# Fused attention and a two-layer feed-forward block: attention ahead of two passes of seven block products that share PSUM banks

## The chip, the cores and the metric

The kernel runs on one NeuronCore of a Trainium2 chip, as one program. The metric is device time in microseconds (us) of one execution, the median of three runs: 921.73 us for the kernel before (920.55 to 922.61). Everything is computed in fp32 or in pairs of fp32r halves.

## The reference

```python
scores = cap * np.tanh((q @ k.T / sqrt(64)) / cap)      # 4 batches x 12 heads, 448 x 64
attn = exp(scores - max); attn /= attn.sum(-1) + 1e-9
x = concat_heads(attn @ v)                              # (4, 448, 768)
u = x + ((x.T @ U @ V).T)                               # mixing over the 448 tokens, rank 32
out = u + np.maximum(u @ w_ch1, 0) @ w_ch2              # w_ch1 768 x 3072, w_ch2 3072 x 768
```

The weights U, V, w_ch1 and w_ch2 arrive as 64-bit floats and are turned into fp32 on the chip.

## The kernel before

A small planner inside the program makes a list of tasks (each with an engine or a choice of two, a duration, a priority, and the buffers it uses), plays them through in time, and writes the instructions out in the order found. So every engine gets a fixed queue, and what the planner was told (durations, latencies, priorities, begin times, pools of buffers) sets the order. A task that may go to ScalarE (ACT) or VectorE (DVE) is given to one of them there.

**Attention** (`two`, `normalize`, `mixin`) goes in 12 steps of two head pairs (four heads). Scores (line 396) are 64-row fp32 products, two at a time on TensorE (PE); ACT takes tanh (401) and exp (409); the products with v (436) and the product for the last 64 keys (423, "rest") go into `o` banks; DVE adds the exponentials (445), PE sums them over partitions (475), and the reciprocal makes a round trip through DRAM on the POOL queue (480, 485, 498) before u is scaled (502). `mixin` transposes u (525), multiplies with U (540) and V (561) and adds (565). PE works in another shape ("mode") for scores, rest, products with v, sums, and everything else. q is scaled on DVE (376). `ALONE = 12` lets the first six steps use extra PSUM banks; the other six begin at planned times (`FROM`, `PACE`) among the feed-forward work.

**The feed-forward part** (`moe`) makes two passes over the 3072 hidden columns in 12 chunks of two blocks of 128. Pass 0 serves batches 0 and 1, pass 1 batches 2 and 3. Every product is three fp32r matmuls (high x high, high x low, low x high) of 448 columns.
- In pass 0, `up_plain` (738) takes 18 matmuls for each of 2 blocks x 2 batches: 72 a chunk.
- In pass 1, `up_seven` (759) multiplies the 2 x 2 blocks of batches and hidden columns by seven block products (Winograd's form of Strassen's scheme): 63 a chunk. The operand sums are made by `operands` and `strassen_weights` (lines 590, 597). Each product gets a PSUM bank of its own; ACT copies two out (229) and DVE does five adds from PSUM (771) and two in SBUF (776).
- `down` (823) takes 72 matmuls a chunk, 6 for each of 12 output tiles, and DVE adds each bank to u (828), 288 adds in all.
- Relu leaves two halves in `g` (229, 723).
- `block` and `convert`: in pass 0 a raw 64-bit block is loaded (623, two `wr` buffers) and made fp32 by one ACT instruction (270) and three DVE instructions (274, 279, 283); the result is used and also stored to DRAM (627, `kept`). Pass 1 loads it from there (617). DVE and ACT split each block into halves (654, 229).

At the end of pass 1 the 12 outputs are sent to DRAM (834).

Of the kernel before, what the change touches and what calls it, by code (L numbers as in the profile page):

```python
# [11 lines left out]
F32 = mybir.dt.float32  # L12
F32R = mybir.dt.float32r
# [6 lines left out]
DM = H * D  # L20
# [13 lines left out]
ALONE = 12  # L34

PACE = 50000
FROM = 90000
# [27 lines left out]
LAT = {"PE": 240, "ACT": 110, "DVE": 110, "POOL": 150, "SP": 0}  # L65
SWITCH = 95


class Plan:
# [43 lines left out]
    def simulate(self):  # L113
# [11 lines left out]
        def room(b):  # L125
            if self.order[b.tag][head[b.tag]] is not b:
                return None
            for p in b.pools:
                if p.free[b.tag] and all(not q.due for q in p.after):
                    return p  # L130
            return None

        def can(t, e):
            if any(b.pool is None and not room(b) for b in t.bufs):
                return False
# [10 lines left out]
        def start(t, e):  # L146
# [6 lines left out]
            cost = t.durs[e] + (SWITCH if t.mode != mode[e] else 0)  # L153
# [11 lines left out]
        while True:  # L165
            for e in LAT:
                if free[e] <= now and ready[e]:
                    for t in sorted(ready[e], key=lambda t: (t.prio, t.i)):
                        if can(t, e):
                            start(t, e)  # L170
                            break
            if not events:
                break
# [61 lines left out]

class Build(Plan):
    def __init__(self, tc, qk, v, u, vv, w1, w2, cap, ident, out):
# [7 lines left out]
        self.wp = Pool("wp", {"wa": 2, "w1": 3, "g": 3})  # L245
        self.wq = Pool("wq", {"wr": 2, "w0": 2})
        self.pre = Pool("pre", {"th": 4, "qk": 1, "es": 2})
        self.hp = Pool("hp", {"hl": 2}, after=(self.pre,))
        self.ap = Pool("ap", {"qk": 3, "vn": 2, "th": 3, "es": 2, "sr": 1, "r7": 2, "rb": 2, "xh": 1, "xl": 1, "ys": 1},
            side="right")  # L250
        self.xp = Pool("xp", {"x": 4, "ws": 3, "g": 3, "wa": 1}, after=(self.hp, self.wq))
        self.late = Pool("late", {"x": 3, "ws": 4, "cx": 4, "ta": 3}, after=(self.ap,), side="right")
        self.px = Pool("px", {"sc": 1, "s": 1}, space=PSUM, side="right")
        self.ps = Pool("ps", {"sc": 1, "o": 1, "misc": 2}, space=PSUM)
        self.pm = Pool("pm", {"mm": 3}, after=(self.px,), space=PSUM, side="right")
        self.pl = Pool("pl", {"mm": 5}, after=(self.ps,), space=PSUM)
        self.dp = None


    def convert(self, raw, raw_t, a, a_t, prio, n):  # L260

        nc = self.nc
        k = n / 768
# [4 lines left out]
        def low():  # L272
            half = raw_t().bitcast(U16)
            nc.vector.tensor_scalar(  # L274
                out=half[:, 0::4], in0=half[:, 1::4], scalar1=13, scalar2=None, op0=ALU.logical_shift_right)
# [10 lines left out]

        self.task({"ACT": 900 * k}, absolute, r=[(raw, "u")], w=[(a, 0)], prio=prio)
        self.task({"DVE": 1040 * k}, low, r=[(raw, "l")], w=[(raw, "l0")], prio=prio)
        self.task({"DVE": 1040 * k}, sign, r=[(raw, "u"), (raw, "l0")], w=[(raw, "l1")], prio=prio)
        self.task({"DVE": 960 * k}, join, r=[(raw, "l0"), (raw, "l1"), (a, 0)], w=[(a, 0)], prio=prio, lock=True)  # L290


    def consts(self):
# [6 lines left out]
        nc.vector.tensor_scalar(out=self.qsc, in0=self.qsc, scalar1=1.0 / D ** 0.5, scalar2=None, op0=ALU.mult)  # L300
        self.ident = pool.tile([128, 128], F32, name="ident")
# [5 lines left out]
    def mixing_consts(self):  # L307
        nc = self.nc
        begin, prio = 4000, -150
        raw = self.buf("wr", [128, 2 * DM], I32, self.wq)  # L310
        raw2 = self.buf("wr", [128, 2 * DM], I32, self.wq)
        a, a2 = (self.buf("wa", [128, DM], F32, self.wp) for _ in range(2))
# [25 lines left out]
        self.task({"DVE": 800}, u_parts, r=[(a, 0)], w=[("ust", 0)], prio=prio)  # L338
        self.convert(raw2, lambda: raw2.t[:, :2 * S], a2, lambda: a2.t[:, :S], prio, S)
        self.task({"DVE": 900}, v_parts, r=[(a2, 0)], w=[("vst", 0)], prio=prio)  # L340


    def attention(self):

        self.u_bufs = [self.buf("u%d" % b, [128, NP, S], F32, self.up) for b in range(B)]
        for p in range(0, B * NP, 2):
            self.two(p)
            self.normalize(p + 1)  # L350
            self.mixin(p // NP, p % NP // 2)

    def psum(self, tag, p, n=1):
        pools = {"sc": (self.ps, self.px), "s": (self.px,)}.get(tag) if p < ALONE else None
        tag = "misc" if tag == "s" and not pools else tag
        return self.buf(tag, [128, 512] if n == 1 else [128, n, 512], F32, *(pools or (self.ps,)))

    def begin(self, p):
        return 0 if p < ALONE else FROM + (p - ALONE) // 2 * PACE

    def two(self, p):


        nc = self.nc
        b, prio = p // NP, p - 100
        begin = self.begin(p)
        pools = (self.ap, self.pre) if p < ALONE else (self.ap,)
        vn = self.buf("vn", [128, 7, 2, D], F32, self.ap)
        qks = [self.buf("qk", [128, 2, S], F32, *pools) for _ in range(2)]
        for i, qk in enumerate(qks):  # L370

            def load(i=i, qk=qk):
                nc.sync.dma_start(out=qk.t, in_=self.qk[b, p % NP + i])

            def scale(qk=qk):
                nc.vector.tensor_scalar(out=qk.t[:, 0], in0=qk.t[:, 0], scalar1=self.qsc, scalar2=None, op0=ALU.mult)  # L376

            self.task({"SP": 350}, load, w=[(qk, 0)], lat=3600, prio=prio, begin=begin)
            self.task({"DVE": 560}, scale, r=[(qk, 0)], w=[(qk, 0)], prio=prio)
# [513 lines left out]
```

## Time and profile before

| what | value |
|---|---|
| median of three runs | 921.73 us |
| the profiled execution: span | 921.8 us |
| PE busy | 898.0 us (97%) |
| DVE busy | 714.1 us (77%) |
| ACT busy | 379.9 us (41%) |
| matmuls, attention and mixing / pass 0 / pass 1 | 1080 / 1728 / 1620 |
| mean granted PE clock | 0.992 of 2.4 GHz |

The profile is of one execution. Busy time is the union of an engine's instructions; a matmul's record is longer than the time until the next can start, so the chain's pieces, which run from start to start, are the better price of a group of matmuls. The span of the profile and the median of the runs agree to 0.1 us.

### The profile page before, as it was taken

How to read it: one execution, taken by the hardware profiler on the slowest of the kernel's cores; microseconds unless marked ns; L12 is line 12 of the kernel's file. 1: busy time of each engine (PE TensorE's matmuls, PEld its weight loads, DVE VectorE, ACT ScalarE, POOL GpSimd, SP SyncE). 2: the span in 40 equal slices, each digit the busy share in tenths (PEclk: the TensorE clock that was granted, in tenths of full speed). 3: DMA queues.
4: the chain of work that ended last, by engine and by line, in shares of the span. 5: the costliest groups of instructions: out<-in, count | busy, mean ns of one | idle time of the engine just before them, and what ended most of it. 6: DMA issues, size and time to landing. Idle time of an engine off the chain costs nothing.

```text
span 921.8 us, 11491 instructions
## 1 busy us (share of the span) xinstructions
PE 898.0 (97%) x4428; PEld 704.5 (76%) x4428; DVE 714.1 (77%) x1119; ACT 379.9 (41%) x513; POOL 60.5 (7%) x112
## 2 busy tenths in 40 slices
PE   6999999999999998999999999899999999999998
PEld 2233375767767666599999998799999999999997
DVE  5798896887887876778898775977777777777755
ACT  6988755545354541724323232512332222332210
POOL 0322210101011111020000000000000000000000
PEclk9999999999999998999999999999999999999999
DMA  7546330545434426145445433221121121122103
GB/s 255 173 153 204 92 101 32 163 175 169 167 125 149 138 61 211 66 137 181 121 156 190 163 103 123 100 72 67 52 69 56 48 61 60 52 69 67 38 1 120
DMA packets 34262, 104.58 MB, mean 113 GB/s; under 512 B 6192, under 2 KB 10272, under 8 KB 34208
## 3 DMA queue, kind: packets, MB, share of 16 engines
q1 hardware_dynamic: 23072, 79.29, 27.6%
q10 hardware_dynamic: 6912, 18.88, 5.1%
q0 software_dynamic: 4224, 5.68, 2.2%
q8 instruction: 35, 0.57, 0.3%
q14 instruction: 19, 0.16, 0.1%
HBM read 79.28 MB, written 24.47 MB: 113 GB/s over the span
## 4 chain that ended last, share of the span: by engine, by line
PE 90%; DMA 4%; DVE 4%; issue 1%; ACT 1%; POOL 0%; SPq 0%; DVEq 0%; POOLq 0%
PE mm L823 37%; PE mm L738 18%; PE mm L759 15%; PE sc L396 7%; PE o L436 4%; PE misc L436 2%; PE o L423 2%; PE misc L540 2%; DMA qk<-in_qk 1%; PE misc L525 1%; DMA r<-sr 1%; DMA rb<-rd 1%; DMA rd<-r 1%; PE misc L561 1%; PE misc L475 1%
## 5 line engine op out<-in xcount | busy, mean ns | idle before, releaser
L823 PE MATMUL mm<-g,w 128*128 128x448 f32 x1728 | 376.3, 368 | 0.5 <-DVE g L723 0.4
L823 PEld LDWEIGHTS mm<-g,w 128*128 128x128 f32 x1728 | 322.3, 188 | 44.5 <-issue 8.2
L828 DVE TENSOR_TENSOR u<-u,mm 128x448 f32<-128x448 f32 x288 | 177.7, 622 | 54.5 <-PE mm L823 50.5
L738 PE MATMUL mm<-hl,w 128*128 128x448 f32 x864 | 189.4, 371 | 0.0
L738 PEld LDWEIGHTS mm<-hl,w 128*128 128x128 f32 x864 | 160.2, 189 | 28.9 <-issue 14.9
L759 PE MATMUL mm<-x,ws 128*128 128x448 f32 x756 | 166.4, 368 | 3.7 <-DVE ws L597 3.6
L759 PEld LDWEIGHTS mm<-x,ws 128*128 128x128 f32 x756 | 142.4, 189 | 16.9 <-DVE ws L597 4.4
L401 ACT ACTIVATE th<-sc 128x896 f32<-128x896 f32 x84 | 75.2, 917 | 57.5 <-PE sc L396 43.4
L396 PE MATMUL sc<-qk 64*128 64x448 f32 (+1 forms) x384 | 87.1, 595 | 7.3 <-DVE qk L376 6.1
L229 ACT ACTIVATE w<-wa 128x768 fp32r<-128x768 f32 x72 | 59.4, 838 | 57.3 <-PE mm L823 35.7
L409 ACT ACTIVATE th<-th,capt 128x1792 f32<-128x1792 f32 (+1 forms) x48 | 76.7, 1603 | 0.7
L771 DVE TENSOR_TENSOR cx<-cx,mm 128x448 f32<-128x448 f32 x60 | 37.2, 620 | 45.8 <-PE mm L759 45.8
L654 DVE TENSOR_TENSOR w<-wa,w 128x768 fp32r<-128x768 f32 x72 | 68.6, 952 | 1.3 <-ACT w L229 0.3
L270 ACT ACTIVATE wa<-wr 128x768 f32<-128x768 f32 (+2 forms) x50 | 44.8, 896 | 55.7 <-DVE w L654 43.1
L274 DVE TENSOR_SCALAR wr<-wr 128x768 uint16<-128x768 uint16 (+2 forms) x50 | 50.6, 1024 | 17.1 <-DMA wr<-in_w 14.9
L396 PEld LDWEIGHTS sc<-qk 64*128 64x128 f32 (+1 forms) x384 | 27.1, 178 | 41.9 <-issue 14.7
L445 DVE TENSOR_TENSOR es<-es,th 128x896 f32<-128x896 f32 (+1 forms) x48 | 52.1, 1084 | 6.8 <-ACT th L409 6.3
L229 ACT ACTIVATE ws<-ta 128x384 fp32r<-128x384 f32 x39 | 20.3, 523 | 75.6 <-PE mm L759 69.3
L279 DVE TENSOR_SCALAR wr<-wr 128x768 uint16<-128x768 uint16 (+2 forms) x50 | 50.7, 1022 | 0.2
L229 ACT ACTIVATE g<-mm 128x448 fp32r<-128x448 f32 x48 | 26.1, 543 | 60.1 <-PE mm L738 60.1
L436 PE MATMUL o<-th,vn 128*64 128x448 f32 x216 | 47.5, 561 | 3.3 <-ACT th L409 3.0
L283 DVE SCALAR_TENSOR_TENSOR wa<-wa,wr 128x768 int32<-128x768 int32 (+2 forms) x50 | 46.5, 931 | 2.6 <-ACT wa L270 2.4
(77 smaller groups left out, 597.3 us busy)
## 6 DMA issues: line engine op xcount, KB each, us to landing
wr<-in_w SPq DMA_DIRECT2D x48, 768.0 KB, 5.5
kept<-wa ACTq DMA_DIRECT2D x48, 384.0 KB, 5.7
wa<-kept SPq DMA_DIRECT2D x48, 384.0 KB, 3.1
qk<-in_qk SPq DMA_DIRECT2D x24, 448.0 KB, 5.8
vn<-in_v SPq DMA_DIRECT2D x12, 448.0 KB, 7.3
rb<-rd POOLq DMA_DIRECT2D x48, 112.0 KB, 3.8
out_t<-u SPq DMA_DIRECT2D x24, 224.0 KB, 1.9
r<-sr POOLq DMA_DIRECT2D x48, 1.8 KB, 2.7
```

What stands on the lines that cost most here:

```text
L229: e.activation(out=out, in_=in_, func=func)
L279: nc.vector.tensor_scalar(out=half[:, 1::4], in0=half[:, 3::4], scalar1=0x8000, scalar2=None, op0=ALU.bitwise_and)
L396: nc.tensor.matmul(ps.t[out, a, :S], qks[c].t[hd, 1, 128 * t:min(S, 128 * t + 128)], qks[c].t[hd, 0], start=True, stop=True)
L401: nc.scalar.activation(out=th.t[:, j], in_=ps.t[:, :, :S], func=AF.Tanh)
L409: nc.scalar.activation(out=th.t[:, :n], in_=th.t[:, :n], func=AF.Exp, scale=self.capt)
L436: nc.tensor.matmul(o.t[64 * a:64 * a + 64, :S], vn.t[:, 3 * i + t, a], th.t[:, j, a], start=t == 0 and not late, stop=t == 2 and late)
L445: e.tensor_tensor(out=out(), in0=in0(), in1=in1(), op=ALU.add)
L654: e.tensor_tensor(out=w.t[:, 1], in0=a.t, in1=w.t[:, 0].bitcast(F32), op=ALU.subtract)
L738: nc.tensor.matmul(ps.t[:, :S], w.t[:, wi, sl], hl.t[:, xi, d], start=d == 0 and i == 0, stop=d == ND - 1 and i == 2)
L759: nc.tensor.matmul(ps.t[:, :S], ws[p].t[:, wi, sl], xs[p].t[:, xi, d], start=n == 0, stop=n == 8)
L823: nc.tensor.matmul(ps.t[:, :S], w1[f].t[:, wi, sl], g[b, f].t[:, gi], start=f == fs[0] and i == 0, stop=f == fs[-1] and i == 2)
L828: nc.vector.tensor_tensor(out=u.t[:, d], in0=u.t[:, d], in1=ps.t[:, :S], op=ALU.add)
```

## The change

- **Order.** All 12 attention steps come first with the extra banks (`ALONE = 22`), the begin times are gone, and mixing runs two steps behind (`LAG`). The planner's durations and latencies are replaced, a change of PE's mode has a price of its own, and among PE tasks within two priorities of the best one that keeps the mode is taken (`NEAR`).
- **Attention.** q is not scaled on DVE; tanh takes the scale. The rest product is one task for both head pairs in all steps.
- **Passes.** Both passes use `up_seven`. Products 1, 6, 7 and 4 are accumulated in one PSUM bank (`chain`) and products 5 and 3 in a second; the bank is read between them: three ACT copies and three DVE adds from PSUM a chunk, and one relu directly from the bank.
- **Down.** 3 of the 12 output tiles (`STAY`) keep a PSUM bank for the whole pass and are added to u once, at its end: 222 adds in all. Five banks are left for the others.
- **Weights.** `converted` runs as its own stream, begun at 9 us and planned no closer than 7 us apart, with one `wr` and one `wc` buffer (two in the first eight blocks); the low part may be made on ACT (`FLOOR`). Both passes load the blocks from DRAM.

```diff
-ALONE = 12
-PACE = 50000
-FROM = 90000
+ALONE = 22
+LAG = 2
+STAY = 1, 5, 9
+FIRST = 8
+START, PACE = 9000, 7000
+NEAR = 2
...
+        self.cv = Pool("cv", {"wr": 1, "wc": 1})
+        self.pre = Pool("pre", {"th": 4, "qk": 1, "es": 2, "wr": 1, "wc": 1})
...
+        self.pl = Pool("pl", {"mm": 5 - len(STAY), "acc": len(STAY)}, after=(self.ps,), space=PSUM)
...
-                    nc.scalar.activation(out=th.t[:, j], in_=ps.t[:, :, :S], func=AF.Tanh)
+                    nc.scalar.activation(out=th.t[:, j], in_=ps.t[:, :, :S], func=AF.Tanh, scale=self.qsc)
...
-        if late:
-            self.task({"PE": 760}, lambda: rest((0, 1)), r=[(vn, 0), (rth, rj)], w=[(o, 0) for o in os], prio=prio, mode="ar")
+        self.task({"PE": 760}, rest, r=[(vn, 0), (rth, rj)], w=[(o, 0) for o in os], prio=prio, mode="ar")
...
-            xs = self.operands(bs) if n else {b: self.halves(b) for b in bs}
+            xs = self.operands(bs, -50)
...
+        product(1, chain, True, False)
+        keep(chain, "c11")
         yield
+        ps = self.bank()
+        product(2, ps, True, True)
+        plus("c11", ps)
         result(0, 0, "c11")
         yield
+        ps = self.bank()
+        product(5, ps, True, False)
+        keep(ps, "c22")
         yield
+        product(6, chain, False, False)
+        keep(chain, "c12")
         yield
+        product(3, ps, False, True)
+        plus("c12", ps)
         result(0, 1, "c12")
         yield
+        product(7, chain, False, False)
+        plus("c22", chain)
+        result(1, 1, "c22")
         yield
+        product(4, chain, False, True)
+        self.relu(bs[1], fs[0], lambda: chain.t[:, :S], (chain, 0), gs)
         yield
...
+                stay = k in STAY
+                if stay and c == 0:
+                    self.stay[k] = self.buf("acc", [128, 512], F32, self.pl)
+                ps = self.stay[k] if stay else self.bank()
...
+                if last or not stay:
+                    self.task({"DVE": 538}, add, r=[(ps, 0)], w=[(u, d)], prio=-200)
...
+        self.task({"SP": 350}, load, w=[(raw, "u"), (raw, "l")], lat=4800, prio=prio, begin=START + PACE * (len(self.raws) - 1))
```

What the change does to the queues is read at three places. The first is PE in the attention stage of the kernel before, about the time of the fifth step; sc are scores, o products with v (436) and rest (423), the misc rows the mixing of an earlier step.

```order
L436 MATMUL o<-th,vn 64x448 x4
L525 MATMUL misc<-ident,u_193 112x128 x4
L396 MATMUL sc<-qk 128x448 x4
L540 MATMUL misc<-xh,ust 128x256 x2
L436 MATMUL o<-th,vn 64x448 x2
L540 MATMUL misc<-xl,ust 128x256 x2
L525 MATMUL misc<-ident,u_193 112x128 x4
L423 MATMUL o<-th,vn 64x448 x2
L396 MATMUL sc<-qk 128x448 x2
```

The same of the changed kernel, a few steps later (line 417 scores, 455 products with v, 443 rest, 491 sums, 540 to 576 mixing).

```order
L491 MATMUL misc<-es,ones 32x448 x4
L540 MATMUL misc<-ident,u_550 112x128 x4
L417 MATMUL sc<-qk 64x448 x4
L417 MATMUL sc<-qk 128x448 x2
L555 MATMUL misc<-xh,ust 128x256 x2
L555 MATMUL misc<-xl,ust 128x256 x2
L540 MATMUL misc<-ident,u_550 112x128 x4
L417 MATMUL sc<-qk 128x448 x4
L555 MATMUL misc<-xh,ust 128x256 x2
L555 MATMUL misc<-xl,ust 128x256 x2
L443 MATMUL o<-th,vn 64x448 x4
L455 MATMUL o<-th,vn 64x448 x4
```

Pieces of one mode stand together more often now: over the whole queue PE changes mode 205 times before and 148 times after, and rest is one group of four a step.

The second place is PE where the last attention step ends. Before, the last sums (line 475) stand in the middle of pass 0, among its down (823) and up (738) matmuls.

```order
L823 MATMUL mm<-g,w_2668 128x448 x3
L823 MATMUL mm<-g,w_2836 128x448 x3
L475 MATMUL misc<-es,ones 32x448 x4
L738 MATMUL mm<-hl,w_2736 128x448 x18
L738 MATMUL mm<-hl,w_2940 128x448 x18
```

In the changed kernel they stand at the start of pass 0: line 728 is a block product of nine matmuls, and the misc rows are the mixing of the last three steps.

```order
L728 MATMUL mm<-x,ws 128x448 x9
L491 MATMUL misc<-es,ones 32x448 x4
L540 MATMUL misc<-ident,u_1472 112x128 x4
L728 MATMUL mm<-x,ws 128x448 x9
L555 MATMUL misc<-xh,ust 128x256 x2
L555 MATMUL misc<-xl,ust 128x256 x2
L540 MATMUL misc<-ident,u_1472 112x128 x4
L728 MATMUL mm<-x,ws 128x448 x9
L555 MATMUL misc<-xh,ust 128x256 x2
L555 MATMUL misc<-xl,ust 128x256 x2
L728 MATMUL mm<-x,ws 128x448 x9
```

So pass 0 begins as the attention ends, with the block products of its first chunk between the last mixing groups.

The third place is DVE in the middle of pass 0, where raw weight blocks become fp32. Before, four blocks pass in a chunk, and two are in work at once (274, 279 and 283 are the three instructions of a block).

```order
L274 TENSOR_SCALAR wr<-wr 128x768
L828 TENSOR_TENSOR u_555<-u_555,mm 128x448
L279 TENSOR_SCALAR wr<-wr 128x768
L828 TENSOR_TENSOR u_555<-u_555,mm 128x448
L654 TENSOR_TENSOR w_4194<-wa,w_4194 128x768
L274 TENSOR_SCALAR wr<-wr 128x768
L283 SCALAR_TENSOR_TENSOR wa<-wa,wr 128x768
L723 SCALAR_TENSOR_TENSOR g<-mm,g 128x448
L279 TENSOR_SCALAR wr<-wr 128x768
```

In the changed kernel (306, 311 and 315 are the three, 796 the adds of down, 741 those of the block products, 710 relu's low half) one block is in work at a time.

```order
L306 TENSOR_SCALAR wr<-wr 128x768
L741 TENSOR_TENSOR cx<-cx,mm 128x448
L311 TENSOR_SCALAR wr<-wr 128x768
L710 SCALAR_TENSOR_TENSOR g<-cx,g 128x448
L796 TENSOR_TENSOR u_550<-u_550,mm 128x448
L315 SCALAR_TENSOR_TENSOR wc<-wc,wr 128x768
L608 TENSOR_TENSOR ws<-wa,ws 128x384 x2
L741 TENSOR_TENSOR cx<-cx,mm 128x448
L796 TENSOR_TENSOR u_550<-u_550,mm 128x448
L710 SCALAR_TENSOR_TENSOR g<-cx,g 128x448
L796 TENSOR_TENSOR u_550<-u_550,mm 128x448
L667 TENSOR_TENSOR w_3063<-wa,w_3063 128x768
```

Of the 48 blocks, 14 are done when the last row sum of the attention is added; the other 34 pass in pass 0, three in each chunk.

## Rows read from the trace of the kernel before

**Rows 1.** The page, busy time by engine.
```profile
PE 898.0 (97%) x4428; PEld 704.5 (76%) x4428; DVE 714.1 (77%) x1119; ACT 379.9 (41%) x513; POOL 60.5 (7%) x112
```

**Rows 2.** By stretch: span, busy PE, PEld, DVE, ACT, POOL (instructions), clock, DMA, GB/s.
```profile
0.00:20.00 20.00, 12.38 (x52) 4.35 (x52) 9.75 (x24) 12.71 (x13) 0.20 (x4) 1.00 0.81 269
20.00:100.00 80.00, 78.25 (x416) 28.35 (x414) 68.93 (x95) 71.47 (x78) 22.62 (x40) 1.00 0.52 165
115.00:363.00 248.00, 243.21 (x1217) 171.64 (x1216) 194.35 (x277) 118.08 (x147) 29.65 (x54) 1.00 0.41 135
500.00:550.00 50.00, 50.00 (x247) 45.81 (x246) 38.68 (x54) 15.68 (x22) 0.00 (x0) 1.00 0.43 138
550.00:600.00 50.00, 46.04 (x222) 41.32 (x221) 39.98 (x75) 18.20 (x34) 0.00 (x0) 1.00 0.32 107
640.00:667.50 27.50, 27.50 (x136) 25.34 (x135) 21.09 (x38) 7.51 (x13) 0.00 (x0) 1.00 0.19 58
```

**Rows 3.** The chain in order of time (start, length, what): feed-forward pieces.
```profile
423.87 7.30 PE mm L738 x36
...
903.42 14.60 PE mm L823 x72
```

**Rows 4.** The chain, attention pieces of PE.
```profile
59.38 1.70 PE sc L396 x8
61.08 2.40 PE o L436 x12
63.49 0.95 PE sc L396 x4
...
70.31 0.90 PE o L436 x4
71.21 0.90 PE o L423 x4
...
189.33 0.52 PE o L423 x2
189.86 0.01 PE misc L423 x2
```

**Rows 5.** PE in order of time: first and last of six groups of sums.
```profile
27.19 0.96 PE L475 MATMUL s<-es,ones 128*32 128x448 f32 x8
...
113.52 0.96 PE L475 MATMUL s<-es,ones 128*32 128x448 f32 x8
```

**Rows 6.** Two groups of ACT by line: count, busy us, mean ns of one, idle before.
```profile
L401 ACT ACTIVATE th<-sc 128x896 f32<-128x896 f32 x84 | 75.2, 917 | 57.5 <-PE sc L396 43.4 <-PE o L436 13.8
L409 ACT ACTIVATE th<-th,capt 128x1792 f32<-128x1792 f32 x36 | 64.4, 1789 | 0.6
```

**Rows 7.** DVE in order of time: attention, then a raw block in pass 0.
```profile
60.82 1.08 DVE L445 TENSOR_TENSOR es<-th 128x896 f32<-128x896 f32 x1
61.82 0.62 DVE L502 TENSOR_TENSOR u<-u,rb 128x448 f32<-128x448 f32 x1
...
516.82 1.06 DVE L274 TENSOR_SCALAR wr<-wr 128x768 uint16<-128x768 uint16 x1 [2.84 <-DMA wr<-in_w]
```

**Rows 8.** The chain: DRAM round trip of one reciprocal, from copy to multiplication.
```profile
336.41 0.56 ACT sr L229
...
343.64 6.36 DMA rd<-r
...
350.81 6.68 DMA rb<-rd
...
357.51 0.62 DVE u L502
```

**Rows 9.** DMA issues of the whole run: count, KB each, median us from issue to landing.
```profile
rb<-rd POOLq DMA_DIRECT2D x48, 112.0 KB, 3.8
...
rd<-r POOLq DMA_DIRECT2D x12, 7.0 KB, 2.5
```

**Rows 10.** The tile wr, 440 to 520 us.
```profile
DMA to landing us min/median/max: 5.2/5.6/6.6
```

More of the change, by code (lines that the diff above doesn't have):

```diff
@@ L123, in simulate, with room, roomy @@
                 heapq.heappush(events, (t.begin, 0, t.i, "r"))
-        def room(b):
-            if self.order[b.tag][head[b.tag]] is not b:
+        def room(b, before=()):
+            same = [x for x in before if x.tag == b.tag]
+            if self.order[b.tag][head[b.tag] + len(same)] is not b:
                 return None
+            n = len(same)
             for p in b.pools:
-                if p.free[b.tag] and all(not q.due for q in p.after):
-                    return p
-            return None
+                if all(not q.due for q in p.after):
+                    if p.free[b.tag] > n:
+                        return p
+                    n -= p.free[b.tag]
+            return None
+        def roomy(t):
+            new = [b for b in t.bufs if b.pool is None]
+            return all(room(b, new[:i]) for i, b in enumerate(new))
         def can(t, e):
-            if any(b.pool is None and not room(b) for b in t.bufs):
+            if not roomy(t):
                 return False
@@ L152, in start @@
                     head[b.tag] += 1
-            cost = t.durs[e] + (SWITCH if t.mode != mode[e] else 0)
+            cost = t.durs[e] + (SWITCH[t.mode] if t.mode and t.mode != mode[e] else 0)
             mode[e] = t.mode
@@ L415, in two, with rest @@
         self.es = getattr(self, "es", {})
-        os = [self.psum("o", p), self.psum("o" if p < ALONE else "misc", p)]
-        late = p >= ALONE
-        def rest(pairs):
-            for i in pairs:
+        os = [self.psum("o", p), self.psum("o2", p)]
+        def rest():
+            for i in range(2):
                 rows = slice(64 * i, 64 * i + 64)
@@ L676, in bank @@
-    def bank(self, late):
-        return self.buf("mm", [128, 512], F32, *((self.pm, self.pl) if late else (self.pm,)))
-    def moe(self):
-        self.kept = {}
+        self.task({"ACT": 734}, high, r=[(a, 0)], w=[(w, 0)], prio=prio)
+        self.task({"DVE": dve(DM)}, low, r=[(a, 0), (w, 0)], w=[(w, 1)], prio=prio)
+        return w
+    def bank(self):
+        return self.buf("mm", [128, 512], F32, self.pm, self.pl)
+    def moe(self):
+        self.kept, self.raws, self.stay = {}, [], {}
+        for c in range(NCH):
+            for which in range(2):
+                for i in range(CF):
+                    self.converted(which, c * CF + i, 2)
@@ L691, in moe @@
                 gs = {}
[L692 to L700 removed]
+                down = self.down(order, *pend) if pend else iter(())
+                if c == 0 and pend:
@@ L701, in moe @@
                     for _ in down:
                         pass
[L703 to L714 removed]
+                    order += 12
@@ L715, in moe, with relu @@
+                for _ in self.up_seven(bs, fs, xs, ws, gs, order):
+                    next(down, None)
+                    next(down, None)
+                for _ in down:
+                    pass
+                pend = bs, fs, w1, gs, c
+                order += 20
         for _ in self.down(order, *pend):
             pass
-    def relu(self, b, f, src, key, gs, late):
+    def relu(self, b, f, src, key, gs):
         nc = self.nc
-        g = gs[b, f] = self.buf("g", [128, 2, S], F32R, *((self.wp, self.xp) if late else (self.wp,)))
+        g = gs[b, f] = self.buf("g", [128, 2, S], F32R, self.lt, self.le)
@@ L764, in product, with keep @@
                 prio=next(at), mode="mm")
[L766 to L772 removed]
+        def keep(ps, x):
+            self.task({"ACT": 440}, lambda: self.copy(nc.scalar, cx[x].t, ps.t[:, :S]), r=[(ps, 0)], w=[(cx[x], 0)],
```

319 lines of the change are left out of this document (129 added, 190 removed).

## The prediction

> **What bounds the kernel now.** I read the busy times first. TensorE (PE) is busy for 898.0 of the span's 921.8 us [rows 1], so it is idle for 23.8. The windows say where [rows 2]: 7.6 in the first 20 us (first loads and first exponentials), 1.75 from 20 to 100, 4.8 from 115 to 363, 4.0 from 550 to 600, where the passes change, and none from 500 to 550 or from 640 to 667.5. The last matmul ends at 918.02 (903.42 + 14.60), which leaves 3.8 for the last add and store [rows 3]. So 11.4 lies at the two ends and 12.4 between. Then I read the chain: it is almost all PE, and a feed-forward matmul takes 0.203 us whichever tile it writes (7.30 / 36 for up, 14.60 / 72 for down) [rows 3]. The kernel is bound by PE: the end moves by PE work that goes, by changes of PE's mode that go, and by waits that PE gains. The other engines come near a bound only in the attention stage: from 20 to 100 us ACT is busy for 71.5 of 80 and DVE for 68.9 [rows 2].
>
> **The change, part by part.** PE work that goes is on the path in full.
>
> 1. Block products in pass 0: 12 chunks of 72 up matmuls become 12 of 63, 108 fewer. 108 x 0.203 = -21.9 us.
> 2. Rest products: in the first six steps each of two head pairs has its own group, 0.90 us with its change of mode [rows 4]; now both share one. The later steps have that form already, and there the second pair's matmuls (`misc`) start beside the first pair's, at 0.01 of the chain after 0.52 [rows 4]. 6 x 0.90 = -5.4; bounds -5.4 and 0.
> 3. Mode changes: 205 in PE's queue before, 148 after; six of the 57 are in part 2. Price: two score groups apart cost 2 x 0.95, together 1.70, so 0.20; three groups of products with v cost 3 x 0.90 apart, 2.40 together, so 0.15 for each of the two changes saved [rows 4]. 51 x 0.17 = -8.7, bounds -7.7 and -10.2.
>
> Together -36.0. Nothing of PE's work is added: the three kept output tiles and the shared banks leave its matmuls as they are. The 24 scalings of q, 66 adds to u, and the adds in the block products go from DVE, which does not set the end; I cost them at nothing, and they are the cover for part 7.
>
> Then the waits, against 12.4 between the ends before.
>
> 4. Attention by itself. Up to its last row sum DVE's queue holds 274 instructions, about 208 us by their mean durations; up to the last exponential ACT's holds 208 compute instructions, about 202 us, 77.0 of it tanh (84 x 0.917) and 64.4 long exponentials (36 x 1.789) [rows 6]. Records overlap: an add that takes 1.08 is followed after 1.00 [rows 7], so 0.08 goes off each, and DVE needs 186, ACT 185. PE's queue up to the last sums: 12 steps x 15 groups of 0.75 (1.70 less 0.20, halved) are 135, mixing 20.5, changes of mode 22, and 36 block matmuls of the first chunk 7.3: 185. So three engines of equal load go side by side, where before PE led and lost 1.75 in 80. I take twice that rate over 180 us: 7.9. Bounds: 0, and the 17 of the first rival.
> 5. The seam to pass 0. The last steps' reciprocal goes through DRAM. The trip on the chain took 21.7 (336.41 to 358.13), with 6.36 and 6.68 for two of its DMAs [rows 8], where the medians are 2.5 and 3.8 [rows 9]; at the medians it would be 15.0. Between the last sums and the last step's transposes PE's queue holds 36 block matmuls (7.3) and the mixing of two earlier steps (about 6). PE waits for 1.5 to 8.2; I take 2, by the medians.
> 6. The change of passes keeps its form: operand sums of the next pass are made by DVE while the last outputs are added. 4.0 as before [rows 2]; bounds 1 and 10.
> 7. Shared banks. PE may not go on in a bank before the copy out of it is done. Between products 1 and 6 and between 6 and 7 two or more other products' work stands; between 7 and 4 only two down groups, 12 x 0.203 = 2.44 us, against an add of 0.62 [rows 7] and what DVE has in hand, at most about 1.0. It fits, except in the first chunk of each pass, where no down group stands between: 0.9 together.
> 8. Raw weight blocks in pass 0. A block now has one buffer, so the next load waits for the last instruction on the block before: 5.6 to landing [rows 10], three instructions of about 0.95, and some 0.8 for what stands between them in the queue: 9.3, three in a chunk 27.8, against 27.5 for a chunk [rows 2]. DVE will wait for loads, but it has waited before (2.84 at 516.82) [rows 7] with PE never idle between 500 and 550 [rows 2]. DVE's load in a chunk is 18 us of feed-forward and 8.5 of raw blocks, some 40 overlaps of 0.08 taken off: 23.3 of 27.5. I take 0; bounds 0 and the 66 of the slow rival.
>
> Waits between the ends: 7.9 + 2 + 4.0 + 0.9 = 14.8, 2.4 more than before. 921.8 - 36.0 + 2.4 = 888.2; the profiled span and the median of the runs agree to 0.1, so I forecast 888 us, with 880 to 896 as its own range.
>
> Two rules are weighed here. From 115 to 363 us attention lies among feed-forward work: ACT is busy for 48% and DVE for 78% there, and PE still loses 4.8 us [rows 2]; in the stage of attention alone PE loses no larger share. The Trainium skill (Perfetto Trace Analysis, Optimization Strategy) says that stretches with different busiest engines can gain from being interleaved, and this change takes them apart. By that rule the attention stage would fall to the pace of ACT and DVE, which is the first rival; the trace of 20 to 100 us speaks against it, at a lower load than now.
>
> No row before shows a bank that is read and then written further. The Trainium skill (PSUM — Partial Sum Buffer, PSUM bank collisions raise a hardware error) says that PE must not write a bank while another engine reads it, and that nothing but a semaphore keeps them apart; so each read in the middle is a wait of PE's, and part 7 decides whether it is covered. Where it isn't, the bank rival holds.
>
> **The rivals.**
>
> - *Attention paced by all three engines.* Six groups of sums from 27.19 to 113.52 are 17.3 us a step [rows 5]. If a step keeps that pace, the twelfth sums start at 27.2 + 11 x 17.3 = 217.5 instead of 185 + 7.6 + 7.9 = 200.5: 17 more, 905 us. For it: equal load on three engines in fixed queues. Against: a step held two rest groups and more changes of mode then.
> - *Fewer waits than I take.* The seam is covered, the three engines mesh, the change of passes costs 1: 888 - 12 = 876 us.
> - *Banks.* DVE comes about 1 us late to the read before product 4 in each chunk: 22 x 1 = 22, so 910 us. For it: DVE is nearly full in pass 0. Against: reads have the highest priority.
> - *Slower: the raw stream sets pass 0.* If reloads of finished blocks, new in pass 0, stand before the raw loads, the landing goes to 6.6 [rows 10] or beyond; with 1.0 more for a reload ahead a block takes 11.3 and a chunk 33.9, 6.4 more than PE needs. From the second chunk to the last but one that needs raw blocks (10.3 chunks): 66 us, so 954. It decides from 10.3 us a block (3.4 x 10.3 = 35 us, no gain left). For it: one buffer, and DVE's queue is fixed, so a late landing holds the adds behind it. Against: the ten loads from 440 to 520 us land within 6.6 [rows 10], at four blocks in 144 x 0.203 = 29.2 us.
> - *The change doesn't do what it says*, because attention and pass 0 lose what the block products save: about 920.
>
> **How the numbers follow.** My forecast has 0.41, fewer waits 0.19, paced attention 0.20, banks 0.07, the raw stream 0.09, no effect 0.04. The range 869 to 912 holds the first four but for their outer ends, 0.80 or a little more. A measurement of this kernel tells about 0.2% (1.8 us) from no change: faster 0.87, within it 0.03, slower 0.10 (the raw stream, and some of the last case).
>
> **What would show it.** In the changed profile: 3240 feed-forward matmuls at 0.203 each, the last sums of attention at about 200 us, chunks of 27.5 us in both passes, PE busy for about 862. The last sums at 217 would show paced attention; waits of PE's for the adds of block products, in every chunk, the banks; chunks of 29 or more in pass 0 alone, with DVE waiting for raw loads, the raw stream. The forecast is wrong in its mechanism if PE's busy time falls by less than 30 us, or if PE is idle for more than 40.

## The result and the profile after

The changed kernel takes 934.97 us (933.91 to 936.24, 4 runs) beside 922.17 for the kernel before (920.55 to 924.62, 4 runs) on the same chip: 1.0137 of its time, 95% interval 1.0118 to 1.0156. It is slower by 1.4%, clear of the noise; 888 with a range of 869 to 912 was forecast. The profiled execution has a span of 932.1 us, 10.3 more than before. In the experiments below, one of the four executions of run 8, the profiled one, took 1945.27 us, with a granted clock of 0.16 from 680 us on: its trace is read only up to there, and the time of run 8 is that of the other three.

The page answers [rows 1]: busy time by engine, and PE's share of it in 40 slices, the clock under it.

```profile
PE 875.0 (94%) x4320; PEld 686.9 (74%) x4320; DVE 710.7 (76%) x1153; ACT 443.7 (48%) x623; POOL 59.3 (6%) x112
...
PE   6879999889598999999999999899999999999998
...
PEclk9999999999799999999999999999999999999999
```

PE's busy time fell by 23.0, but the rest of the span, PE idle, rose from 23.8 to 57.1: -23.0 + 33.3 = +10.3. So the work did go, and waits took more than it gave. The windows, to set beside [rows 2] (same columns), say where.

```profile
20.00:100.00 80.00, 69.82 (x378) 24.16 (x376) 66.34 (x83) 71.86 (x74) 19.69 (x36) 0.98 0.67 220
100.00:150.00 50.00, 48.33 (x258) 18.38 (x257) 44.46 (x66) 47.40 (x53) 13.81 (x27) 1.00 0.58 194
150.00:200.00 50.00, 46.00 (x256) 18.22 (x254) 47.32 (x76) 46.68 (x53) 13.49 (x26) 1.00 0.35 108
200.00:250.00 50.00, 39.66 (x195) 23.10 (x191) 42.25 (x64) 32.83 (x44) 12.13 (x20) 0.93 0.48 147
250.00:300.00 50.00, 45.12 (x213) 39.65 (x214) 40.92 (x68) 19.33 (x32) 0.00 (x0) 0.94 0.50 159
...
450.00:500.00 50.00, 47.89 (x231) 42.75 (x230) 42.11 (x67) 20.15 (x35) 0.00 (x0) 1.00 0.57 189
500.00:550.00 50.00, 48.05 (x233) 43.22 (x233) 40.12 (x66) 19.19 (x29) 0.00 (x0) 1.00 0.53 171
550.00:600.00 50.00, 44.64 (x214) 40.33 (x213) 47.10 (x88) 20.37 (x37) 0.00 (x0) 0.98 0.33 112
640.00:667.50 27.50, 27.50 (x138) 25.43 (x137) 17.57 (x31) 8.19 (x15) 0.00 (x0) 1.00 0.20 58
```

PE loses 10.2 of 80 us from 20 to 100, where it lost 1.75 before; 10.3 of 50 from 200 to 250, where pass 0 begins; about 2 in every 50 through pass 0, where it lost none from 500 to 550; 5.4 where the passes change, 4.0 before; and none in pass 1. A mark for each stage comes from PE in order of time: the last row sums of the attention, to set against the forecast of 200.5.

```profile
228.22 0.96 PE L491 MATMUL misc<-es,ones 128*32 128x448 f32 x8
```

Busy times hide what a matmul loses while its record stays open. I therefore also took every matmul's start in both traces: where the next one starts over 0.3 us later than after the quickest of the same kind, the excess is a stall. By that count all stalls are 22.7 us before and 65.9 after: 33.0 up to the last sums, 12.0 from there to the second chunk at 254.3, 14.9 in the rest of pass 0, 6.0 in the change of passes, none in pass 1. The remainder between the first matmul and the last, PE's own work with its changes of mode, fell from 889 to 857.

ACT by line (count, busy, mean of one, idle before), against [rows 6]:

```profile
L422 ACT ACTIVATE th<-sc,qsc 128x896 f32<-128x896 f32 x84 | 82.2, 1022 | 8.7 <-PE sc L417 6.7 <-PE o L455 2.0
...
L304 ACT ACTIVATE wr<-wr 128x768 uint16<-128x768 uint16 x11 | 21.3, 1939 | 14.4 <-DMA wr<-in_w 14.4
```

Tanh with its scale read from a column takes 1022 ns, 917 before. The low part of a raw block, which the planner was told takes 804 ns on ACT, takes 1939. Both made the attention stage suspect, and were the first to be tried.

In pass 0 it is 28.6 to 29.7 us from a chunk's first product to the next one's, from the third chunk on, and in pass 1 27.4. The chain in order of time (start, length, what) shows the loop in pass 0:

```profile
534.84 0.88 DVE wc L315
...
535.74 6.26 DMA wr<-in_w
...
542.09 0.06 DVE wr L306
...
542.94 0.67 DVE cx L741
543.61 0.91 DVE wr L311
...
545.54 0.88 DVE wc L315
...
546.47 5.28 DMA wr<-in_w
```

This is one raw block after another: the load may start when the last instruction on the block before (315) is done, and DVE works the block through with its adds between. Once round is 10.7 us here; three blocks fill a chunk of 29.2, so 9.7 on average. The tile wr from 300 to 550 us, what it waited for, who waited for it, and its loads ([rows 10]):

```profile
  DMA wr<-in_w: 44.3, 28
...
  DVE wr L306: 24.3, 18
...
DMA to landing us min/median/max: 5.2/5.5/6.3
```

DVE (306) waits for raw loads 18 times, 24.3 us together, in these 250 us; in the kernel before it did so 19 times for 14.9 us in the 435 us from 115 to 550:

```profile
  DVE wr L274: 14.9, 19
```

How that reaches PE is seen at one of its stalls. PE in order of time:

```profile
380.36 1.38 PE L791 MATMUL mm<-g,w 128*128 128x448 f32 x6
383.00 1.28 PE L791 MATMUL mm<-g,w 128*128 128x448 f32 x5 [1.26 <-DVE cx L741]
```

and DVE's queue ahead of that stall:

```profile
376.10 1.06 DVE L306 TENSOR_SCALAR wr<-wr 128x768 uint16<-128x768 uint16 x1 [1.14 <-DMA wr<-in_w]
...
377.52 1.04 DVE L311 TENSOR_SCALAR wr<-wr 128x768 uint16<-128x768 uint16 x1
378.65 0.96 DVE L315 SCALAR_TENSOR_TENSOR wc<-wc,wr 128x768 int32<-128x768 int32 x1
379.52 0.61 DVE L796 TENSOR_TENSOR u<-u,mm 128x448 f32<-128x448 f32 x1
380.06 0.55 DVE L601 TENSOR_TENSOR ta<-wa 128x384 f32<-128x384 f32 x1
...
382.33 0.61 DVE L741 TENSOR_TENSOR cx<-cx,mm 128x448 f32<-128x448 f32 x1
```

The add that PE waits for (741) needs nothing of the raw block; it stands behind it in a queue whose order is fixed. By the name of the releaser this would be a wait for a shared bank; the wait further up DVE's queue points at the raw stream, which runs 5, 8 and 9 test.

### The profile page after: what moved, and what is told of

Same layout as the page of the kernel before. It is cut to its first block, busy times and chain, and to the rows that moved or that the text cites. A ratio compares the mean times of both kernels' runs of the same rounds, so it can differ in the third digit from the quotient of the medians.

```text
span 932.1 us, 11540 instructions
## 1 busy us (share of the span) xinstructions
PE 875.0 (94%) x4320; PEld 686.9 (74%) x4320; DVE 710.7 (76%) x1153; ACT 443.7 (48%) x623; POOL 59.3 (6%) x112
## 5 line engine op out<-in xcount | busy, mean ns | idle before, releaser
L728 PE MATMUL mm<-x,ws 128*128 128x448 f32 x1512 | 334.7, 369 | 10.3 <-DVE ws L608 5.4
L728 PEld LDWEIGHTS mm<-x,ws 128*128 128x128 f32 x1512 | 284.1, 189 | 40.2 <-DVE cx L741 7.9
L791 PE MATMUL mm<-g,w 128*128 128x448 f32 x1296 | 288.7, 367 | 7.2 <-DVE cx L741 6.7
L791 PEld LDWEIGHTS mm<-g,w 128*128 128x128 f32 x1296 | 242.2, 188 | 31.2 <-DVE cx L741 9.3
L791 PE MATMUL acc<-g,w 128*128 128x448 f32 x432 | 99.2, 365 | 0.0
L417 PE MATMUL sc<-qk 64*128 64x448 f32 (+1 forms) x384 | 82.9, 596 | 15.7 <-ACT th L422 10.7
L422 ACT ACTIVATE th<-sc,qsc 128x896 f32<-128x896 f32 x84 | 82.2, 1022 | 8.7 <-PE sc L417 6.7
L791 PEld LDWEIGHTS acc<-g,w 128*128 128x128 f32 x432 | 81.0, 188 | 6.8
L299 ACT ACTIVATE wc<-wr 128x768 f32<-128x768 f32 (+2 forms) x50 | 45.3, 906 | 60.5 <-DMA kept<-wc 44.6
L608 DVE TENSOR_TENSOR ws<-ta,ws 128x384 fp32r<-128x384 f32 x96 | 53.6, 560 | 4.8 <-ACT ws L254 3.9
L315 DVE SCALAR_TENSOR_TENSOR wc<-wc,wr 128x768 int32<-128x768 int32 (+2 forms) x50 | 47.0, 940 | 2.6 <-ACT wc L299 1.3
```

The costliest lines, as they stand in the source:

```text
L315: nc.vector.scalar_tensor_tensor(out=a_t().bitcast(I32), in0=a_t().bitcast(I32), scalar=3, in1=raw_t()[:, 0::2], op0=ALU.logical_shift_lef ...
L417: nc.tensor.matmul(ps.t[out, a, :S], qks[c].t[hd, 1, 128 * t:min(S, 128 * t + 128)], qks[c].t[hd, 0], start=True, stop=True)
L422: nc.scalar.activation(out=th.t[:, j], in_=ps.t[:, :, :S], func=AF.Tanh, scale=self.qsc)
L608: e.tensor_tensor(out=lo, in0=src(), in1=hi.bitcast(F32), op=ALU.subtract)
L728: nc.tensor.matmul(ps.t[:, :S], ws[p].t[:, wi, sl], xs[p].t[:, xi, d], start=first and n == 0, stop=n == 8, skip_group_check=True)
L791: nc.tensor.matmul(ps.t[:, :S], w1[f].t[:, wi, sl], g[b, f].t[:, gi], start=fresh and f == fs[0] and i == 0, stop=done and f == fs[-1] and ...
```

## The experiments

Each kernel is the changed one with the edit shown, unless said otherwise. Positions of the last sums are read like the row above; some kernels place block products of the first chunk ahead of them, at 0.203 us each, which I take off where stages are compared ("net": 228.2 - 36 x 0.203 = 220.9 for the changed kernel). Each position is of one execution; the changed kernel and runs 5, 8 and 9, whose attention holds the same work, lie between 220.9 and 225.5 net, so a difference of less than 5 us between two such positions says little.

**1. Tanh with its scale as a number.**

```diff
- ... func=AF.Tanh, scale=self.qsc)
+ ... func=AF.Tanh, scale=1.0 / (30.0 * D ** 0.5))
```

> Tanh takes its scale as a number written into the instruction (1/240) instead of from a column in SBUF; all else as in the changed kernel. Theory A (attention is paced by ACT, and the column costs it 0.105 us on each of 84 tanh): tanh falls from 1022 to about 917 ns, the last sums come 6 to 9 us earlier than 228.6, the whole is 6 to 9 us shorter than the 935 of the changed kernel. Rival B (the three queues of equal load mesh badly, whatever a single instruction costs): last sums within 3 us of 228.6. Rival C (the time lies in the seam and in pass 0): last sums may move, the end by less than 3.

Tanh fell to 926 ns, the last sums came at 227.7, and the kernel took 933.30 us, ratio 1.0142 (1.0111 to 1.0173). 84 x 0.096 = 8 us less on ACT bought 1.7 us at most, as rival B had it: tanh's length does not set the pace.

**2. No low parts on ACT.**

```diff
-FLOOR = 1
+FLOOR = 0
```

> FLOOR = 0: the low part of a raw block is always made by DVE (11 of 48 were made by ACT, at 1.94 us each where the planner was told 0.80). Theory A: ACT loses 5 x 1.94 = 9.7 us before the last sums, DVE gains 5 x 0.84 = 4.2; last sums 3 to 8 us earlier, the whole 3 to 8 us shorter. Rival B: last sums within 3 us of 228.6. In pass 0 DVE gains 6 x 0.84 = 5 us of work over 295 us; chunks stay at 29 to 30 us by either.

926.37 us, ratio 1.0047 (1.0030 to 1.0064): 8.6 us of the loss. The last sums come at 220.5 with 18 block products ahead, net 216.8, 4.1 earlier, which is within the scatter of positions; the second chunk starts at 245.8, 8.5 earlier (in the changed kernel at 254.3), so 4.4 are won at the seam between the last sums and there. The chunks of pass 0 stay at 29.0.

**3. Both edits.**

```diff
- ... func=AF.Tanh, scale=self.qsc)
+ ... func=AF.Tanh, scale=1.0 / (30.0 * D ** 0.5))
-FLOOR = 1
+FLOOR = 0
```

> The number in tanh and FLOOR = 0 together. Theory A: ACT is about 18 us lighter before the last sums; they come 10 to 16 us earlier, at 213 to 219, and the end moves by as much, to about 920. Rival B: last sums at 222 or later.

923.53 us, ratio 1.0028 (1.0008 to 1.0049), which can't be told from the second alone. The last sums come at 222.9, net 219.3: not the 213 to 219 of theory A, but rival B's mark.

**4. The planner is told both true durations.**

```diff
-        self.task({"DVE": 1.08 * n, "ACT": 190 + 0.8 * n} if FLOOR else ...
+        self.task({"DVE": 1.08 * n, "ACT": 1665} if FLOOR else ...
...
-                self.task({"ACT": 800}, tanh, ...
+                self.task({"ACT": 890}, tanh, ...
```

> The instructions cost what they did; only the planner is told the true spacing of tanh (890 instead of 800 ns) and of the low part on ACT (1665 instead of 804), so that it gives fewer copies and low parts to ACT and orders by what will happen. Theory A: ACT has less to do in attention, the last sums come 4 to 9 us earlier. Rival B (fixed queues hold each other up because the plan's times are wrong): the last sums come earlier too, by 8 or more, since the order then fits. If neither: within 3 us.

945.36 us, ratio 1.0259 (1.0221 to 1.0297): a miss. The last sums come at 223.6, 4.6 us earlier, but in the new order 59.0 us lie between the first products of the last chunk of pass 0 and those of pass 1 (44.1 in the changed kernel), and the planner still gives ACT 11 low parts. A truer price in a greedy plan moves everything behind it, so this run tells nothing of the price itself.

**5. A short raw stream.**

```diff
-            ... nc.sync.dma_start(out=a.t, in_=self.kept[which, f]),
+            ... nc.sync.dma_start(out=a.t, in_=self.kept[which, f % 8]),
...
-        for c in range(NCH):
+        for c in range(4):
```

> Leaves out 32 of the 48 raw blocks (loads, conversion, store); both passes read the first 16 converted blocks in their place. Attention's queue is as in the changed kernel up to two or three instructions. Theory D (the raw stream, one buffer, 9.7 us a block, sets the pace of pass 0): chunks of pass 0 fall from 29.2 to 27.4 us from the third on, some 16 to 20 us, and the end with them, to about 915. Rival E (pass 0 is slow because of shared banks or reloads): chunks stay above 28.5.

910.95 us, ratio 0.9875 (0.9847 to 0.9903). The last sums stay (230.2), and in pass 0 every stall is gone:

```profile
300.00:550.00 250.00, 250.00 (x1234) 231.24 (x1233) 164.15 (x294) 75.09 (x132) 0.00 (x0) 1.00 0.18 56
```

The chunks take 27.4 as in pass 1, with the same shared banks and the same three kept output tiles. So it is the raw blocks that make these chunks longer. Whether it is their stream or DVE's work on them this run doesn't tell (DVE is busy for 164 of the 250 us, in the changed kernel for 206); run 8 does. The second chunk takes 32.2 even so, in the changed kernel 32.9.

**6. The kernel before, with its attention first.** Raw blocks, passes and mode order as before.

```diff
-ALONE = 12
+ALONE = 24
```

> The kernel before with one number changed (ALONE = 24): attention first, alone, and then the old two passes; the raw blocks but five pass in pass 0, as they did. Theory F (taking attention out of pass 0 is the loss, as by the rule of interleaving): attention's 12 steps take 17.3 us each, last sums at about 217; the feed-forward work after it is 351 + 330 + about 8 us of waits; end at 905 to 915, a little under 922: the interleaving was worth nothing. If interleaving hid work: 935 or more.

915.93 us, ratio 0.9938 (0.9905 to 0.9971): attention ahead of the passes, with the extra PSUM banks for all its steps, is a gain. Its stage, with 6 raw blocks in it:

```profile
20.00:200.00 180.00, 179.00 (x928) 63.99 (x930) 148.03 (x209) 152.88 (x162) 52.34 (x94) 1.00 0.44 141
```

PE leads here and loses 1.0 of 180; the changed kernel loses 15.9 in the same stretch, with DVE and ACT 10 and 13 us busier. The last sums come at 211.2, with no block product ahead: earlier than expected (217), and earlier than the net 220.9 of the changed kernel.

**7. No raw block in the attention.**

```diff
-FIRST = 8
-START, PACE = 9000, 7000
+FIRST = 0
+START, PACE = 230000, 7000
```

> Raw blocks begin only at 230 us, so that attention has none in its queues (pass 0 then starves, which is not what is looked at). Theory B (three queues of equal load mesh badly): with 14 blocks gone DVE loses 38 us of 186 and ACT 22 of 185, PE leads again, and the last sums come at 200 to 208 instead of 228.6. Rival G (PE's own changes of mode and its waits for scores set the pace): last sums at 218 or later.

One run took 1082.49 us, since pass 0 starves for weights; only its attention is read. PE in order of time, the last four sums:

```profile
205.28 0.95 PE L491 MATMUL misc<-es,ones 128*32 128x448 f32 x4 [0.93 <-DVE es L462]
```

No block product stands ahead of them. The last four sums of the changed kernel start at 228.6, net 221.3: the 15 raw blocks that it finishes by then cost PE 16.0 us, 1.07 each. The stage from 20 to 200 us, to set beside run 6:

```profile
20.00:200.00 180.00, 171.93 (x960) 65.06 (x956) 145.69 (x213) 159.32 (x168) 50.84 (x99) 1.00 0.35 108
```

PE leads again, but still loses 8.1. In pass 0, which now waits for it, the stream took about 10 us a block, four blocks a chunk of 40.

**8. A second raw buffer in pass 0.** Its room comes from the ws pool (5 to 2); the loads of pass 0 are planned 8.2 us apart.

```diff
-        self.lt = Pool("lt", {"ws": 5, "w1": 2, "g": 5}, ...
+        self.lt = Pool("lt", {"ws": 2, "w1": 2, "g": 5, "wr": 1, "wc": 1}, ...
-        pools = (self.cv, self.pre) if len(self.raws) < FIRST else (self.cv,)
+        pools = (self.cv, self.pre) if len(self.raws) < FIRST else (self.cv, self.lt)
```

> A second wr and wc buffer in pass 0, paid for with three ws buffers, and the raw blocks of pass 0 planned 8.2 us apart; the same work in all. Theory D: chunks of pass 0 at 27.4 to 28, the end 12 to 18 us earlier, 917 to 923. Rival E: chunks stay above 28.5, the end moves by less than 5. If DVE's own load in pass 0 (25 of 27.4 us) is the bound: between, 28 to 28.6.

903.79, 906.99 and 911.76 us, ratio 0.9840 (0.9790 to 0.9889). The tile wr from 300 to 550 us:

```profile
  DMA wr<-in_w: 8.0, 6
...
  DVE wr L306: 2.3, 1
...
DMA to landing us min/median/max: 4.4/5.7/7.8
```

The loads land no sooner, but DVE waits for them once, for 2.3 us, where it waited 18 times for 24.3, and PE is busy for 248.0 of the 250 (240.7 in the changed kernel):

```profile
300.00:550.00 250.00, 248.02 (x1206) 224.82 (x1205) 222.34 (x360) 106.99 (x173) 0.00 (x0) 1.00 0.53 183
```

The gain, 23 to 31 us beside 934.97, is larger than expected, and it has two parts. The nine steps from the third chunk's first product to the twelfth's take 27.9 each, 29.2 in the changed kernel: 11.4 us. More was won before, at the seam: 44.9 us pass from the last sums to the third chunk's first product, 58.9 in the changed kernel. The edit also plans the loads later, and from 220.2 to 243.9 no raw block stands in DVE's queue.

**9. Its control: only ws cut from 5 to 2.**

```diff
-        self.lt = Pool("lt", {"ws": 5, ...
+        self.lt = Pool("lt", {"ws": 2, ...
```

> Control for the run with two raw buffers, whose pools also cut the operand-sum buffers of the weights (ws) from 5 to 2. Here only that cut is made, the raw stream keeps its single buffer in pass 0. Theory D (the single-buffered raw stream is what slows pass 0): chunks of pass 0 stay near 29.2 us and the time near 935 (932 to 939). Rival (the gain of that run came from the smaller ws pool, through the order of the queue): 905 to 915.

935.02 us, ratio 1.0133 (1.0104 to 1.0162): as the changed kernel, and the chunks stay at 29.2. So the gain of the eighth run is not the smaller ws pool's. The later begin times have no control. In the chunks they can hardly be the cause, since one buffer with its 9.7 us a block can't keep to 8.2; there it is the buffer. At the seam no run tells the buffer from the begin times.

**10. The second raw buffer, and no low parts on ACT.** The eighth run's edit, and

```diff
-FLOOR = 1
+FLOOR = 0
```

> Two edits together: a second raw buffer in pass 0, and the low part of a raw block on DVE only. Theory (two separate costs, the low part on ACT in the attention stage, about 8 us, and the raw stream in pass 0, about 25): the gains add, last sums near 221 us, chunks of pass 0 near 28, time 895 to 906. Rival (DVE becomes the bound of pass 0 when it makes every low part): chunks of pass 0 stay at 29, time 915 to 925.

906.56 us (903.29 to 913.70), ratio 0.9842 (0.9790 to 0.9894): not faster than the buffer alone, just outside what I expected, and the two gains don't add. The last sums, expected near 221, come at 225.2, net 221.6: no earlier than in the changed kernel. The chunks of pass 0 are down to 26.5 to 29.3 from the third on.

**11. The same, with 9 raw blocks in the attention instead of 14.**

```diff
-... if len(self.raws) <= 14 else 215000 + 8200 * (len(self.raws) - 15))
+... if len(self.raws) <= 9 else 212000 + 7200 * (len(self.raws) - 10))
```

> As the run with two raw buffers and low parts on DVE, but only 9 raw blocks are planned in the attention stage instead of 14, and the other 39 from 212 us on, 7.2 us apart. Theory (each raw block among the attention steps costs PE about 1.5 us, and pass 0 has room for 4 blocks a chunk with two buffers): last sums near 213, chunks of pass 0 below 28.5, time 888 to 900. Rival (DVE cannot take 4 blocks in a chunk of 27.4 us beside its adds): chunks of pass 0 at 29.5 or more, time 905 to 925.

900.17 us (899.59 to 900.87), ratio 0.9763 (0.9743 to 0.9782), the fastest of all and faster than both kernels. The last sums, in order of time, and three windows:

```profile
221.51 0.96 PE L491 MATMUL misc<-es,ones 128*32 128x448 f32 x8
```

```profile
200.00:250.00 50.00, 43.74 (x221) 30.23 (x220) 43.55 (x74) 27.99 (x42) 8.98 (x17) 0.97 0.32 106
...
300.00:350.00 50.00, 49.29 (x241) 44.83 (x241) 46.87 (x75) 20.92 (x35) 0.00 (x0) 1.00 0.65 229
350.00:400.00 50.00, 50.00 (x248) 46.29 (x248) 47.90 (x76) 21.09 (x34) 0.00 (x0) 1.00 0.64 220
```

45 block products stand ahead of the last sums, so net 212.4, 9.2 less than in run 10: 1.8 for each of the five blocks. In pass 0 DVE is busy for 47 to 48 of 50 us and PE still loses next to nothing: a nearly full DVE is no bound here as long as it has the next block in hand.

**12. Mixing one step behind instead of two.**

```diff
-LAG = 2
+LAG = 1
```

> Mixing runs one step behind the attention instead of two, so less of it is left for the seam between the attention and pass 0. Theory (the seam is long because the mixing of three steps, a serial chain through DVE and a DRAM round trip, stands between the block products of the first chunk): chunk 1 starts 3 to 10 us earlier after the last sums than the 26 us of the changed kernel, time 925 to 932. Rival (the seam is long because raw blocks and operand sums share DVE with the mixing): 933 to 938.

952.39 us, ratio 1.0336 (1.0294 to 1.0378): another miss. From the last sums to the second chunk it is now 10.5 us instead of 26.1, but the sums come at 243.3 (net 230.5, with 63 block products ahead), and the second chunk starts at 253.8 (254.3 in the changed kernel). That the mixing can be moved without winning anything speaks against the seam as a cost of the mixing alone. In run 8, with no raw block in DVE's queue there, it is 11.8 us, though with less of the mixing in it. Pass 0 is slower (30.5 a chunk), with 11 of 25 low parts on ACT from 300 to 550, 3 of 26 in the changed kernel.

## Why the prediction was wrong

**Parts 1 to 3, PE's work: right, a little too large.** -36.0 was forecast; by starts PE's work fell by 889 - 857 = 32, in it the 21.9 of the block products. The busy time fell by less (23.0), since a record that waits grows. Of the missing 4, some 1.6 are the clock's, by an estimate: at a granted clock of 0.50 stand 13.0 us of PE's work after and 9.8 before. Both marks that I set for a wrong mechanism were met, a fall of PE's busy time below 30 (23.0) and PE idle for more than 40 (57.1). The first was set on the wrong quantity; the second says what happened.

**The waits: the failed half.** With 22.7 us of stalls before, my +2.4 forecast 25.1. There were 65.9: 40.8 more. With the 4 us missing from PE's work that is the 44 to 45 between 888 and the profiled 932.1.

**Part 4, attention by itself: failed at "three engines of equal load go side by side".** 7.9 us were taken for that, twice the loss rate of a stage where PE led. The last sums came at 228.2 instead of 200.5. By run 7, 16.0 of the 27.7 are the raw blocks, whose time I had put into the queues' sums as if it fitted between. Without them 12 remain. I count PE's work up to the last sums there at 182 us, which holds no block product, where I had 185 - 7.3 = 178: 4 to 5 of the 12. The rest are stalls, 18.0 and 5.0 before the first matmul, for which I had 15.5 together. ACT's two mispriced operations explain little of it: tanh's column next to nothing (run 1), the low parts 4.1 at most (run 2; none in run 10). Run 6 shows the other side: where PE is the longest queue by 26 us, the same stage loses 1.0 in 180 (8 of stalls up to its last sums, by the count of starts). So the runs show the price of the raw blocks in this stage, but not that equal sums alone are the reason: in run 7 PE leads by 12.6 us and still loses 8.1, and what the new order costs by itself was not tested. That each engine's late moments fall on the others when orders are fixed is my reading. The first rival (17 more, sums at 217.5) had the right kind of mechanism, at a lower price.

Two things in the prediction's own working were off here. The mark of 200.5 does not belong to 888: after it, 3204 matmuls at 0.203, the remaining mixing (about 9), the waits that I priced (6.9) and the 3.8 at the end lead to about 871. The 888 started from busy time, which holds some 10 us of stalls inside open records (22.7 by starts, 12.4 idle), and the queue was counted too short. So the 27.7 are not all part of the 44. And the stage of attention alone did not lose "no larger share" than the mixed one: 1.75 of 80 is 2.2%, 4.8 of 248 is 1.9%.

Of the interleaving rule of the Trainium skill (Perfetto Trace Analysis, Optimization Strategy) run 6 shows that taking the regimes apart was not what cost: it gained 6 us. What cost was the reverse, the raw blocks interleaved into a stage whose DVE and ACT were nearly full (47.3 and 46.7 of 50 us from 150 to 200).

**Part 5, the seam: 2 us forecast, 12.0 measured as stalls.** PE in order of time at the start of pass 0:

```profile
240.62 0.68 PE L576 MATMUL misc<-vst,ys 128*128 128x448 f32 x2 [2.98 <-DVE ys L567]
242.36 0.74 PE L540 MATMUL misc<-ident,u 128*112 128x128 f32 x4 [1.06 <-DVE u L580]
243.85 0.79 PE L555 MATMUL misc<-xh,ust 112*128 112x256 f32 x2 [0.75 <-ACT xh L254]
...
250.50 1.11 PE L576 MATMUL misc<-vst,ys 128*128 128x448 f32 x2 [1.75 <-DVE ys L567]
253.21 1.42 PE L540 MATMUL misc<-ident,u 128*112 128x128 f32 x4 [1.60 <-DVE u L518]
```

Only the last of these waits is for the reciprocal's trip (518), the one that I priced. The others name the mixing's own chain, PE to DVE or ACT and back, which I had counted as PE work (about 6 for two steps) and which has no block product beside it in PE's queue here. But the longest, 2.98 for ys (567), is a raw block's, as DVE's queue ahead of it shows:

```profile
238.35 1.03 DVE L311 TENSOR_SCALAR wr<-wr 128x768 uint16<-128x768 uint16 x1 [2.93 <-ACT wr L304]
239.50 0.63 DVE L710 SCALAR_TENSOR_TENSOR g<-cx,g 128x448 fp32r<-128x448 f32 x1
240.15 0.42 DVE L567 TENSOR_TENSOR ys<-misc,ys 32x256 fp32r<-32x256 f32 x1
```

DVE stood for 2.93 us until ACT had made that block's low part (304). By the count of starts the seam's stalls are 12 us in the changed kernel and 8.6 in run 2, which has no low part on ACT. From the last sums to the third chunk, over the same matmuls, they are 14 in the changed kernel and 2 in run 8, which has no raw block in DVE's queue at the seam. So most of them go with the raw blocks and not with the mixing as such; but the order changes with them (30 of the 54 mixing matmuls left stand behind the start of run 8's second chunk, 14 in the changed kernel), and no run keeps it fixed. The clock adds to it:

```profile
242.80:256.40 13.60, 8.49 (x26) 5.83 (x25) 11.96 (x20) 5.28 (x10) 2.07 (x4) 0.50 0.88 256
```

After the first two of these gaps the granted clock stands at 0.50, the lower of its two levels (1.2 of 2.4 GHz), for 13.6 us; in run 8 it is 1.00 from 230 to 242. A block product of nine matmuls takes 3.06 us by its records at 254.28, 2.06 at 229.51.

**Part 6, the change of passes:** 4.0 forecast, 6.0 measured. **Part 7, shared banks: right.** In pass 1 no stall is left, and run 5 shows none from 300 to 550 in pass 0 either once the raw stream is out of the way. The bank rival falls, although PE's stalls name the bank's add; run 11, with DVE nearly full, speaks against it too.

**Part 8, the raw stream: failed at "I take 0".** The sum was nearly right: 9.3 us a block, 27.8 a chunk against 27.5. Measured are 9.7 (5.5 to landing, as [rows 10]; 4.2 for the instructions and what stands between, where I had 3.65), so 29.2 a chunk. But 27.8 against 27.5 already means no reserve. A stream without reserve sets the pace, and every 0.1 us more on a block is 0.3 a chunk. I argued that DVE "has waited before" with PE never idle; in that kernel a second buffer loaded meanwhile. 29.2 - 27.4 over nine chunks is 16, and run 5, without the stream, wins just that; the second chunk is 5.5 too long, but 4.8 in run 5 too, and holds the last of the mixing (to 263.1), so most of that has another cause. A second buffer wins 11.4 of the 16 (run 8). No run shows the 1.0 that my slower rival took for a reload ahead of a raw load: the loads land in 5.2 to 6.3. That rival named this mechanism, but said that it decides only from 10.3 us a block, at which the whole gain is gone. That point took the gains of all other parts as kept. With part 4 and the seam failing too, 9.7 was enough for slower. The gaps of PE that return in each chunk (1.43 us at 383.0, 412.8 and 529.2, by starts) are what the Trainium skill (Perfetto Trace Analysis, Optimization Strategy) calls a consistent bubble, a sign that there may be too few buffers for the next tile; runs 8 and 9 agree, 11.4 us in nine chunks for one buffer.

The chances: slower had 0.10 and happened. Two of the rivals held at once, the paced attention and the raw stream. Each alone still left a gain (905, or 888 + 18); I had given no chance to their sum.

## What to carry to other kernels

When a change makes the engines' queues equally long, or a stream's period equal to what its reader needs, count that as a loss and not as a fit: take the longest queue, and add a tenth of the stage or more (here stalls of 18 and 33 us in 205 and 229) unless one engine clearly leads (8 in 211 in run 6). This is a rule of thumb from one kernel. Where a stall names a cheap add, look up its engine's queue for the wait that stands ahead; and before pieces of work are moved, ask which stage has an engine with room, since 5 raw blocks fewer in the attention, a second buffer to take them later and no low parts on ACT turned 1.4% slower into 2.4% faster.

## What was not expected of the hardware

- The low part on ACT, 128 x 768 halves of 16 bits read and written at a step of four, takes 1939 ns; the fp32 absolute value of the same 768 columns at a step of two takes 924 ns (line 299), and the low part on DVE 1.06 us.
- Tanh from PSUM takes 1022 ns with its scale from a column and 926 with a number. The Trainium skill (ScalarE: Activation LUTs, What ACT_TABLE_LOAD costs) gives about 93 ns for each such pointer; the 96 measured agree, and I had not looked there for the price.
- Reading a PSUM bank in the middle of an accumulation and going on in it, four such reads in a chunk, left no stall of PE's in pass 1 (busy for 27.50 of 27.50 us from 640 to 667.5).
